# Loads of the first batch and of the first feed-forward tile on two queues, in another order

## The chip, the cores and the metric

The kernel runs on one core of a Trainium2 chip. Its engines work side by side, each through its own list of instructions in order: TensorE (PE; its weight loads are shown apart as PEld), VectorE (DVE), ScalarE (ACT), GpSimd (POOL) and SyncE (SP), which here only issues transfers. Transfers issued by SyncE and by GpSimd go through two queues to the same 16 DMA engines. The metric is the device time of one execution in microseconds: a median of 380.05 us over 8 runs, from 379.4 to 381.84.

## What is computed

Attention with a bias over 8 batches, 8 heads, 576 positions and 64 columns, then a gated feed-forward block over the 4,608 tokens that it gives (`d_model` 512, `d_ff` 1536).

```python
scores = scale * np.matmul(q, k.transpose(0, 1, 3, 2))
cum = np.cumsum(np.maximum(s, 0.0), axis=-1)
bias = -(cum[:, :, :, None] - cum[:, :, None, :])
scores = np.where(causal, -1000000000.0, scores + np.minimum(bias, 0.0))
attn = np.exp(scores - np.max(scores, axis=-1, keepdims=True))
attn = attn / (np.sum(attn, axis=-1, keepdims=True) + 1e-09)
x = np.matmul(attn, v)                 # tokens x (heads * columns)
g = x @ w_gate
out = (g * (1.0 / (1.0 + np.exp(-g))) * (x @ w_val)) @ w_out
```

## The kernel before, in words

**Attention.** Work on q and k goes by half batches of 4 heads (`HB`, 16 of them). A half batch is loaded in fp32 (`load_one`, L151: 576 KB each for k and for q), cast to bf16 (`cast_one`, L249; in two halves for half batch 0, `cast_half`, L258) and transposed into the tile `kq`: for half batches 0 to 4 (`NPE` 5) by TensorE (`pe_transpose`, L291, and the copies out of PSUM in `pe_out`, L315), for the rest through a scratch tensor in HBM and a transposing load (`scratch`, L268; `transposes`, L277; `split`, L282). The bias enters the scores as four further rows of `kq`, loaded from the tile `HL` (`aug`, L192, line L197), which is made from `s` by a scan on VectorE (L236 to L242). `kq` has two buffers, taken in turn.

A head's scores are nine products in four pieces (`score_piece`, L350, product L375). ScalarE takes the exponential into `pt` (L388), GpSimd then zeroes what lies above the diagonal by two selects (L391, L396). The values are 15 products (`av_piece`, L403, L413); `av_out` (L421) normalises into `ot`, and for batches 0 and 1 (`XB` 2) TensorE transposes a pair of heads into `XT` (`x_pe`, L456), later batches go through HBM (`x_out`, `x_in`). V is loaded in five parts (`load_v`, L166, rows of 256 B, one fp32 buffer) and cast by `cast_v` (L177).

In batch 0 the four pieces of a head are written into two PSUM tiles of two banks (`wide`), so that two activations of 1,024 and 576 columns serve a head. After batch 0 PSUM is laid out anew as eight single banks (`second_psum`, L134) and each piece has its own activation. `take` and `give` hand out the bank that was released longest ago.

**Feed-forward.** Nine tiles of 512 tokens. `gate_value` (L619) runs over 12 blocks of 128 columns: four gate products (L626), a tanh on ScalarE (L631), a product on VectorE into `pp` (L633), four value products (L641) and the product into `ht` (L649). The first two tiles then run `down_plain` (L664, product L670): four times 12 products. From tile 2 on `down_seven` (L689) saves an eighth of the products with sums of operands. The weights come as bf16 by casting loads of GpSimd (`w_load`, L331, line L342), each matrix in two halves.

**Order.** Everything is written in order by hand. L855 to L928 is batch 0: casts, transposes and bias of half batch 0, then `first_batch`, where the weight loads are issued after heads 1, 4 and 5, the loads of half batches 3 to 5, of V of batch 1 and of the down weights after head 7, and the values of head 0 and 1 after head 6, all others after head 7. `keep_warm` (L877) issues products whose results are not used. From L955 on, the loop over tiles takes one item of the feed-forward after the other, counting `n`; `hook` (L948) puts the preparation of half batches 2 and 3 at given `n`, `pump` advances the attention items (`attn_items`, L546) to a position that grows with `n`, from `n0` on, and `do_later` puts out copies of `split` that were deferred. Within `attn_items`, `side` (L481) and `side_v` (L523) put loads, casts and scratch writes at given heads and pieces, `PREP_AT`, `AV_AT` and `X_AT` the transposes, values and outputs.

SyncE's queue holds all plain loads, the scratch traffic, and the bias rows of half batches 0, 2 and 3; GpSimd's the weights, the other bias rows, the outputs and `xs`.

Of the kernel before, what the change touches and what calls it, by code (L numbers as in the profile page):

```python
# [19 lines left out]
def kernel(  # L20
# [86 lines left out]
    PTP = {0: first, "bufs": 8}  # L107

    with tc.manual_schedule():
# [3 lines left out]
        first_psum = ExitStack()  # L113
        psa = first_psum.enter_context(tc.tile_pool(name="psa", bufs=1, space=PSUM))
        bank = {}
        for i in range(2):
            bank["w", i] = psa.tile([128, 1024], FP32, name=f"wide{i}")
        for i in range(4):
            bank["s", i] = psa.tile([128, 512], FP32, name=f"one{i}")
        released = {key: i - 8 for i, key in enumerate(bank)}  # L120
# [3 lines left out]
        def take(kind="s"):  # L124
            b = min((x for x in bank if x[0] == kind), key=lambda x: released[x])
            assert released[b] < OPEN
            released[b] = OPEN
            return b
# [5 lines left out]
        def second_psum():  # L134
            assert all(x < OPEN for x in released.values())
            at_end = dict(released)
            first_psum.close()
            psb = ctx.enter_context(tc.tile_pool(name="psb", bufs=1, space=PSUM))
            bank.clear()
            released.clear()  # L140
            for i in range(8):
                bank["s", i] = psb.tile([128, 512], FP32, name=f"bank{i}")
                released["s", i] = at_end["w", i // 2] if i < 4 else at_end["s", i - 4]

# [6 lines left out]
        def load_one(hb, name, rs=(0, NR)):  # L151
# [3 lines left out]
            nc.sync.dma_start(  # L155
# [10 lines left out]
        def load_v(b, cs):  # L166
# [3 lines left out]
            for c in cs:  # L170
                n = 128 if c < 4 else TAIL
                nc.sync.dma_start(
                    t[0:n, c, :, :],
                    v[b, :, c * 128 : c * 128 + n, :].rearrange("h p d -> p h d"),
                )
# [10 lines left out]
        NEGS2 = -1.0058441162109375  # L186

# [22 lines left out]
        load_qk(1)  # L210
# [6 lines left out]
        make_identity(nc, ident)  # L217

# [10 lines left out]
        pads(0)  # L229
        init_vt(0)  # L230
        init_vt(1)
        nc.vector.memset(aug_rows(1, 0), 0.0)
        nc.gpsimd.memset(aug_rows(1, 1), 0.0)
# [114 lines left out]
        scs = {}  # L348

        def score_piece(bh, ci):  # L350
            hb, hh = divmod(bh, HB)
            pair = bh < H
            if ci == 0:
                pts[bh] = PTP[0].tile(
                [128, PTW], BF16, tag="pt", bufs=PTP["bufs"], name="pt"
            )
# [3 lines left out]
            if pair:  # L360
                if ci % 2 == 0:
                    bs = take("w")
                    scs[bh] = bs
                else:
                    bs = scs[bh]
                base = (512, 0, 0, 512)[ci]
            else:
                bs = take()
                base = 0
            o = base  # L370
            n = sum(hi - lo for _, lo, hi in CHUNKS[ci])
            sc = view(bs, 1024 if pair else 512)
            for (tj, lo, hi) in CHUNKS[ci]:
# [5 lines left out]
                    start=True,  # L379
                    stop=True,  # L380
                )
                o += w
            if not pair or ci % 2 == 1:
                if pair:
                    c0, W = ((576, 1024), (0, 576))[ci // 2]
                else:
                    c0, W = CHUNK_PT[ci], n
                nc.scalar.activation(pt[:, c0 : c0 + W], sc[:, 0:W], AF.Exp, scale=0.125)  # L388
                give(bs)
            if ci == (1 if pair else 0):  # L390
# [90 lines left out]
        def side(h, step, ci):  # L481
            bh = HB * h + step
            if bh == H + 3 and ci == 1:
                for c in range(5):
                    cast_v(1, c, nc.gpsimd)
            if h >= 3 and h + 3 < NHB and (step, ci) == (0, 1):
                load_qk(h + 3)
            hb = h + 1
            if NPE <= hb < NHB:
                late = hb == NPE  # L490
                if (step, ci) == (0, 1):
                    if late:
                        transposes(hb)
                    aug(hb, GP4)
                first = 1 if hb < NPE + 2 else 0
# [4 lines left out]
            if NPE <= hb < NHB:  # L500
                late = hb == NPE
                if (step, ci) == ((1, 1) if late else (0, 2)):
                    cast_one(hb, "k", nc.scalar)
                if (step, ci) == ((2, 1) if late else (1, 2)):
                    cast_one(hb, "q", nc.scalar)
                if (step, ci) == ((3, 1) if late else (2, 0)):
                    scratch(hb)
                if (step, ci) == (3, 3 if hb == NPE + 1 else 0) and not late:
# [5 lines left out]
            if 2 <= bn < B:  # L514
# [5 lines left out]

        V_AT = {(1, 0): 0, (2, 0): 1, (2, 2): 2, (3, 0): 3, (3, 2): 4}

        def side_v(h, step, ci):  # L523
            bn = h // 2 + 1
            if 2 <= bn < B and h % 2 == 1 and (step, ci) in V_AT:
                cast_v(bn, V_AT[step, ci], nc.scalar if bn > 2 else nc.gpsimd)

        def prep_one(hb, i):
# [3 lines left out]
            for r in range(2):  # L532
                pe_out(hb, nm, g, r, nc.scalar if nm == "k" else nc.vector)

        PREP_AT = {
            2: {(0, 3): 0, (1, 3): 1, (2, 1): 2, (2, 3): 3},
# [5 lines left out]
            H + 5: (H + 2, H + 3), H + 6: (H + 4, H + 5), H + 7: (H + 6,),  # L542
        }
        X_AT = {H + 3: (), H + 5: (H + 1,), H + 6: (H + 3,), H + 7: (H + 5,)}

        def attn_items():  # L546
            for kk in range(H, BH + 2):
                h, step = divmod(kk, HB)
                if kk < BH:
# [5 lines left out]
                    if step == 0 and 3 < h + 1 < NPE:  # L555
# [62 lines left out]

        def gate_value(tt, hps, sus):  # L619
            xt = XT[:, :, (tt % 3) * TT : (tt % 3 + 1) * TT]  # L620
            for ft in range(NFT):
                j, f0 = divmod(ft * 128, WCH)
# [384 lines left out]
```

The softmax here doesn't subtract the row's maximum and nothing guards it: scores larger than these inputs give would overflow.

## Time and profile before

| what | us |
|---|---|
| median of 8 runs | 380.05 |
| the profiled execution's own time | 380.15 |
| its span, first to last instruction | 378.3 |
| first bias rows landed | 10.95 |
| first exponential of batch 0 | 12.06 |
| first gate product of tile 0 | 32.21 |
| first values of batch 1 | 55.9 |

The granted TensorE clock is 1.00 over the whole span. The page gives for each engine its busy time, its share of the span and the count of its instructions; a row of digits shows the busy share of 40 slices of 9.46 us in tenths. The chain of waits follows the work that ended last from step to step: start, length, and the engine, tile and line. A line that begins with DMA is the flight of a transfer. In the DMA view q0 is GpSimd's queue and q1 SyncE's; their lines give packets, MB and the share of 16 engines' time.

### The profile page before, as it was taken

To read this page: it belongs to the slowest core of one execution; us is meant where nothing else is said; L and a number is where in the kernel's file an instruction comes from. 1 tells how busy PE (TensorE), PEld (TensorE's weight loads), DVE (VectorE), ACT (ScalarE), POOL (GpSimd) and SP (SyncE) were. 2 spreads that over 40 slices of the span, in tenths; PEclk is the share of its full clock that TensorE was granted. 3 is DMA by queue.
4 is the path that set the end of the run, shared out by engine and by line. 5 is a ranking of instruction groups with operands and counts; after the bars stand their busy time and mean duration, and the time that the engine had idled before them with its cause. 6 is when DMAs were issued, how large, how long until landed. Compare 5 with 4: busy or idle time off the path is not lost.

```text
span 378.3 us, 8674 instructions
## 1 busy us (share of the span) xinstructions
PE 363.1 (96%) x3246; PEld 230.4 (61%) x3246; DVE 290.3 (77%) x577; ACT 242.3 (64%) x459; POOL 206.5 (55%) x326
## 2 busy tenths in 40 slices
PE   3879999999999999999999999999999999999996
PEld 2666556655555555865586558655875575466465
DVE  7666786557895899769975998589958876985984
ACT  7686788687977777578767885697365523323321
POOL 7584357455364646595558656775675426224320
PEclk9999999999999999999999999999999999999999
DMA  7999999998488996499759665996233023001103
GB/s 251 192 248 263 199 265 268 321 267 173 159 169 272 233 282 187 119 237 295 187 164 284 200 161 159 234 201 158 49 71 114 22 30 128 0 2 68 43 2 111
DMA packets 100729, 64.22 MB, mean 170 GB/s; under 512 B 81888, under 2 KB 85824, under 8 KB 100688
## 3 DMA queue, kind: packets, MB, share of 16 engines
q1 hardware_dynamic: 91248, 46.15, 49.2%
q0 software_dynamic: 9440, 17.53, 18.4%
q8 instruction: 25, 0.41, 0.4%
q14 instruction: 16, 0.13, 0.1%
HBM read 37.90 MB, written 19.86 MB: 153 GB/s over the span
## 4 chain that ended last, share of the span: by engine, by line
PE 85%; DVE 7%; DMA 3%; ACT 2%; issue 1%; DVEq 0%; ACTq 0%; SPq 0%
PE bank L626 22%; PE bank L641 22%; PE bank L711 17%; PE bank L375 9%; PE bank L413 6%; PE bank L670 5%; PE wide L375 2%; DVE pp L633 2%; DVE ht L649 1%; ACT pt L388 1%; DMA xs<-ot 1%; DVE kq L326 1%; PE one L413 1%; DMA kq<-HL 1%; DMA s_sb<-in_s_dram 1%
## 5 line engine op out<-in xcount | busy, mean ns | idle before, releaser
L388 ACT ACTIVATE pt<-bank 128x512 bf16<-128x512 f32 x224 | 106.7, 507 | 26.3 <-PE bank L375 18.1
L626 PE MATMUL bank<-XT,wg 128*128 128x512 bf16 x432 | 110.9, 379 | 0.6 <-DVE pp L633 0.2
L641 PE MATMUL bank<-XT,wv 128*128 128x512 bf16 x432 | 110.9, 379 | 0.0
L631 ACT ACTIVATE th<-bank 128x512 bf16<-128x512 f32 x108 | 64.7, 599 | 58.8 <-PE bank L626 56.9
L633 DVE SCALAR_TENSOR_TENSOR pp<-th,bank 128x512 bf16<-128x512 bf16 x108 | 73.7, 682 | 23.8 <-ACT th L631 23.2
L649 DVE SCALAR_TENSOR_TENSOR ht<-pp,bank 128x512 bf16<-128x512 bf16 x108 | 74.0, 686 | 10.4
L658 POOL TENSOR_TENSOR ht<-ht 128x512 bf16<-128x512 bf16 x35 | 40.4, 1154 | 53.0 <-DVE su L656 52.9
L375 PE MATMUL bank<-kq 128*128 128x128 bf16 (+4 forms) x504 | 67.5, 240 | 0.2 <-DVE ht L649 0.2
L375 PEld LDWEIGHTS <-kq 128*128 128x128 bf16 x576 | 47.0, 100 | 33.0 <-issue 5.1
L641 PEld LDWEIGHTS <-wv 128*128 128x128 bf16 x432 | 38.3, 98 | 35.3
L626 PEld LDWEIGHTS <-wg 128*128 128x128 bf16 x432 | 38.4, 98 | 35.1 <-issue 1.1
L391 POOL TENSOR_SCALAR_AFFINE_SELECT pt<-pt 128x512 bf16<-128x512 bf16 x64 | 41.4, 647 | 32.8 <-ACT pt L388 32.1
L413 PEld LDWEIGHTS <-pt 128*128 128x128 bf16 x960 | 41.0, 98 | 16.6 <-issue 0.7
L413 PE MATMUL bank<-vt,pt 128*128 128x65 bf16 x840 | 41.8, 194 | 0.5 <-DVE ot L430 0.5
L447 POOL DMA_DIRECT2D xs<-ot x24 | 21.7, 906 | 28.1 <-DVE ot L430 28.1
L711 PEld LDWEIGHTS <-ht 128*128 128x128 bf16 x336 | 31.2, 98 | 4.3
L197 POOL DMA_DIRECT2D kq<-HL x52 | 32.1, 619 | 0.1
L430 DVE TENSOR_TENSOR ot<-bank,rc 128x320 bf16<-128x320 f32 x56 | 27.5, 492 | 1.9
L396 POOL TENSOR_SCALAR_AFFINE_SELECT pt<-pt 128x64 bf16<-128x64 bf16 x64 | 17.2, 269 | 18.9 <-ACT pt L388 18.8
L711 PEld LDWEIGHTS <-su 128*128 128x128 bf16 x252 | 23.6, 98 | 3.3
L670 PE MATMUL bank<-wo,ht 128*128 128x512 bf16 x96 | 24.7, 379 | 0.0
L776 POOL TENSOR_TENSOR ysb<-ysb 128x512 f32<-128x512 f32 x12 | 15.2, 1270 | 15.3 <-DVE ysb L770 15.3
(96 smaller groups left out, 397.7 us busy)
## 6 DMA issues: line engine op xcount, KB each, us to landing
rawk<-in_k_dram SPq DMA_DIRECT2D x15, 576.0 KB
rawq<-in_q_dram SPq DMA_DIRECT2D x15, 576.0 KB
rawv<-in_v_dram SPq DMA_DIRECT2D x32, 256.0 KB
out_dram<-ysb POOLq DMA_DIRECT2D x32, 256.0 KB, 3.8
xs<-ot POOLq DMA_DIRECT2D x24, 160.0 KB, 3.9
ks<-ck SPq DMA_DIRECT2D x11, 288.0 KB
qs<-cq SPq DMA_DIRECT2D x11, 288.0 KB
wg<-in_moe_w_gate_dram POOLq DMA_DIRECT2D x2, 768.0 KB, 11.7
```

The lines of the kernel that those rows point to most:

```text
L375: nc.tensor.matmul(sc[:, o : o + w], T[:, 1, e * S + 128 * tj : e * S + 128 * (tj + 1)], T[:, 0, e * S + lo : e * S + hi], start=True, sto ...
L388: nc.scalar.activation(pt[:, c0 : c0 + W], sc[:, 0:W], AF.Exp, scale=0.125)
L391: nc.gpsimd.affine_select(pt[:, 1088:1600], pt[:, 1088:1600], pattern=[[0, 4], [1, 128]], compare_op=ALU.is_ge, fill=zreg, base=0, channel ...
L413: nc.tensor.matmul(av[:, bi * (D + 1) : (bi + 1) * (D + 1)], pt[:, c0 : c0 + 128], VT[b % 2][:, tj, h, :], start=(tj == 0), stop=(tj == bi),)
L626: nc.tensor.matmul(pg, WG[j][:, c, f0 : f0 + 128], xt[:, c, :], start=(c == 0), stop=(c == 3),)
L631: nc.scalar.activation(th, pg, AF.Tanh, scale=0.5)
L633: nc.vector.scalar_tensor_tensor(pp, in0=th, scalar=1.0, in1=pg, op0=ALU.add, op1=ALU.mult)
L641: nc.tensor.matmul(pv, WV[j][:, c, f0 : f0 + 128], xt[:, c, :], start=(c == 0), stop=(c == 3),)
L649: nc.vector.scalar_tensor_tensor(hp[:, 2 * k2 : 2 * k2 + 2, :].rearrange("p a n -> p (a n)"), in0=pp, scalar=0.5, in1=pv, op0=ALU.mult, op ...
L658: (nc.vector if ft == NFT - 1 else nc.gpsimd).tensor_sub(hp[:, 1:3, :], hp[:, 1:4:2, :], hp[:, 0:3:2, :])
L670: nc.tensor.matmul(py, hps[ft // 2][:, 2 * (ft % 2) + half, c0 : c0 + 128], WO[ft // WKO][:, ft % WKO, :], start=(ft == 0), stop=(ft == NF ...
L711: nc.tensor.matmul(ps, lhs(p), rhs(p), start=(first and p == 0), stop=(last and p == NP - 1), skip_group_check=True,)
```

## The change

Loads: q of half batch 1, the first two parts of V of batch 0, k and q of half batches 2 and 3 are issued by GpSimd, between its casts; the bias rows of half batch 1 go to SyncE. The value weights of the first half and both matrices' second halves come in quarters. The down weights are issued at items 12 and 14 of tile 0. V of batch 1 and half batches 4 and 5 follow on SyncE after the bias rows of half batch 3. V of batch 1 is cast one head later, and V of batch 2 is loaded in one go later.

Batch 0: the eight single banks hold from the start. The mask of a head is a product of the identity with a tile `lower` that holds -32768 above the diagonal, accumulated under pieces 0 and 3, and the two selects are gone; four activations serve a head. The values of heads 0 to 4 stand between the scores of heads 4 to 7, and the first three blocks' gate products over three of four rows of `XT` stand ahead of the last pair's transposes. Warm-up products: 32 at the start and twice 10 before the scores, one bank (`spare`) is theirs; those at the end are gone.

Tile 0: preparation of half batch 2 from items 1 to 4 to items 3 to 6, with the second copy of each transposed group one item later (`seconds`); the attention starts at item 7, not 6; the down projection first runs over the first six blocks for all four token groups, then over the other six. Later: casts, scratch write and transposing load of half batch 5 later, values of batch 2 one head later, other items for the deferred copies in tile 2.

```diff
-    PTP = {0: first, "bufs": 8}
+    PTP = {0: first, "bufs": 7}
+    lower = first.tile([128, 512], BF16)
...
-        load_qk(1)
+        load_one(1, "k")
...
+        nc.gpsimd.memset(lower, 0.0)
+        nc.gpsimd.affine_select(
+            lower, lower, pattern=[[0, 4], [1, 128]],
+            compare_op=ALU.is_ge, fill=nc.gpsimd.to_reg(MASKED), base=0, channel_multiplier=-1,
+        )
...
+            masked_here = masked and ci in (0, 3)
+            if masked_here:
+                nc.tensor.matmul(
+                    sc, ident, lower[:, 0:n], start=True, stop=False, skip_group_check=True
+                )
...
-            if bh == H + 3 and ci == 1:
+            if bh == H + 4 and ci == 1:
                 for c in range(5):
                     cast_v(1, c, nc.gpsimd)
-            if h >= 3 and h + 3 < NHB and (step, ci) == (0, 1):
+            if bh == H + 4 and ci == 3:
+                load_v(2, range(5))
+            if h == 4 and (step, ci) in ((0, 1), (2, 1)):
+                load_qk(6 + step // 2)
+            if h >= 5 and h + 3 < NHB and (step, ci) == (0, 1):
                 load_qk(h + 3)
...
+                if late and (step, ci) == (0, 1):
+                    scratch(hb)
+                if late and (step, ci) == (0, 3):
+                    transposes(hb)
...
+            eng = nc.scalar if nm == "k" else nc.vector
+            pe_out(hb, nm, g, 0, eng)
+            seconds.append(lambda: pe_out(hb, nm, g, 1, eng))
 
         PREP_AT = {
-            2: {(0, 3): 0, (1, 3): 1, (2, 1): 2, (2, 3): 3},
+            2: {(2, 0): 0, (2, 2): 1, (3, 0): 2, (3, 2): 3},
...
+            2 * H + 1: (), 2 * H + 2: (2 * H, 2 * H + 1),
...
+            order = [(ts_, j) for ts_ in range(4) for j in range(NWCH)]
+            if tt == 0:
+                order.sort(key=lambda x: x[1])
+            for ts_, j in order:
+                yield from part(ts_, j)
...
+        keep_warm(32)
         cast_half(0, "k", 0, nc.scalar)
         cast_half(0, "q", 0, nc.scalar)
         aug(0, SP4)
-        load_v(0, range(5))
-        load_qk(2)
...
+        row_half("k", 0, nc.scalar)
+        row_half("q", 0, nc.vector)
+        cast_half(0, "k", 1, nc.scalar)
+        cast_half(0, "q", 1, nc.gpsimd)
+        load_one(1, "q", eng=nc.gpsimd)
+        load_v(0, (0, 1), nc.gpsimd)
+        load_v(0, (2, 3, 4))
+        nc.gpsimd.memset(aug_rows(1, 1), 0.0)
+        aug(1, SP4)
+        keep_warm(10)
+        row_half("k", 1, nc.scalar)
+        row_half("q", 1, nc.vector)
+        keep_warm(10)
+        cast_one(1, "k", nc.vector)
+        cast_one(1, "q", nc.vector)
+        for c in range(3):
+            cast_v(0, c, nc.gpsimd)
+        w_load("g", 0)
+        cast_v(0, 3, nc.gpsimd)
+        w_load("v", 0, 0)
+        cast_v(0, 4, nc.gpsimd)
+        for nm in ("k", "q"):
+            load_one(2, nm, eng=nc.gpsimd)
+        w_load("v", 0, 1)
+        for nm in ("g", "v"):
+            w_load(nm, 1, 0)
+        load_one(3, "k", eng=nc.gpsimd)
+        scores(0)
+        half_batch("k")
+        scores(1)
+        half_batch("q")
+        scores(2)
+        scores(3)
...
+        aug(2, SP4)
+        cast_one(2, "k", nc.gpsimd)
+        cast_one(2, "q", nc.gpsimd)
+        load_one(3, "q", eng=nc.gpsimd)
+        for nm in ("g", "v"):
+            w_load(nm, 1, 1)
+        init_vt(1)
+        scores(4)
+        values(0, 1)
+        scores(5)
+        values(2, 3)
+        scores(6)
+        values(4)
+        x_pe(0, nc.vector)
+        scores(7)
+        aug(3, SP4)
+        load_v(1, range(5))
+        load_qk(4)
+        load_qk(5)
+        values(5)
+        x_pe(1, nc.vector)
+        values(6)
+        x_pe(2, nc.scalar)
+        values(7)
+        for ft in range(3):
+            products("g", ft, XT[:, :, 0:TT], range(3))
+            if ft == 0:
+                x_pe(3, nc.scalar)
+        give(spare)
...
+        for i in range(4):
+            at_item(3 + i, prep_one, 2, i)
+        at_item(11, cast_one, 3, "k", nc.gpsimd)
+        at_item(12, cast_one, 3, "q", nc.gpsimd)
+        at_item(12, w_load, "o", 0)
+        at_item(14, w_load, "o", 1)
...
-            n0 = 6 if tt == 0 else 0
+            n0 = 7 if tt == 0 else 0
...
-                if i >= 2 * NFT or i % 4 == 1:
+                if i >= 2 * NFT or (i % 4 == 1 if tt != FIRST7 else i % 4 == 3 and i > 3):
                     do_later(1)
+                while seconds:
+                    seconds.pop(0)()
```

`scores(h)` runs the four pieces of a head, `values(*hs)` `av_piece` and `av_out` of each head, `row_half` and `half_batch` the transposes and copies of a half of half batch 0 and of k or q of half batch 1, and `products` begins a block's gate or value products or goes on with those begun.

## The prediction

> **What bounds it now.** I read the page's shares first, then the slices, then the chain of waits in order of time, then the DMA view by window, and last the landings that the trace's semaphore events give. Profiled execution: span 378.3 us, time 380.15 us, 0.10 us above the median of 380.05; so a change of the span carries over to the median as it is.
>
> ```profile
> PE 363.1 (96%) x3246; PEld 230.4 (61%) x3246; DVE 290.3 (77%) x577; ACT 242.3 (64%) x459; POOL 206.5 (55%) x326
> ...
> PE   3879999999999999999999999999999999999996
> ...
> DMA  7999999998488996499759665996233023001103
> ```
>
> TensorE is full from the fourth slice (from about 38 us) to the end, and the DMA engines are full from the second slice to the ninth (9.5 to 85 us). So only the first 35 us hold much TensorE time to win, and there a second resource, the DMA engines, is full as well. Laying each matmul's columns against the distance of the starts, TensorE stands without work for 24 us between its first and last matmul, 13 of them before 32 us; later the only gaps above 0.2 us are 0.34, 0.37, 0.38 and 0.26 us between 32 and 50 us, and 0.28 and 0.63 us at 136 to 138 us.
>
> ```profile
> 7.92 3.02 DMA kq<-HL
> 10.95 0.05 issue
> 10.99 1.05 PE wide L375 x6
> 12.04 0.02 issue
> 12.06 1.03 ACT pt L388
> ...
> 17.44 1.03 ACT pt L388
> 18.47 0.04 issue
> 18.51 0.62 PE wide L375 x6
> ...
> 31.52 0.65 ACT XT L468
> 32.17 0.04 issue
> 32.21 1.04 PE bank L626 x4
> ```
>
> Here the reader sees the start as three links: the bias rows arrive (10.95), eight heads of exponentials run on ScalarE (12.06 to 27.57, a new head every 1.71 us with one hole of 1.9 us), then a tail of values, outputs and transposes until tile 0's first gate product (32.21).
>
> **Part by part. Bias rows.** By the semaphore events k1 landed at 9.60 us, q1 at 11.03 and head 0's bias rows at 10.95: the bias packets waited behind q1, on the same queue. The change issues q1 from GpSimd after GpSimd's cast (8.23 to 8.89), so the bias waits for k1 alone: 9.7 instead of 10.95. TensorE must still pass the second half's transposes (q's cast ends at 8.89; nine of them took 1.17) and ten warm-up matmuls (0.6), which ends near 10.2, and the first exponential then starts at 10.8 instead of 12.06. **-1.25** (ends: -0.2 if the transposes keep their first speed, -1.5).
>
> **Heads.** Four activations of one head in separate banks took 1.69 us (start of the first to end of the last, row at 39.95 us) against 1.71 for two wide ones: nothing. The mask as a matmul adds 576 columns per head, 0.24 us by 0.216 us for 512, 1.9 us in all; ScalarE hides it, busy 9.39 of 10.16 us from 17.44 to 27.6, while TensorE's part of one head (1,600 columns, 0.67, and the mask, 0.24) fits in 1.7 us. Without that cover it would cost 1.9. GpSimd is rid of sixteen selects in batch 0 (8 x (0.63 + 0.23) = 6.9 us), which pays for ten more issues of 0.6 to 0.9 us each (seven loads and three more pieces of weights; four bias rows go to SyncE, at 0.62 each there, with no load behind them until heads 0 to 3 are scored). Holes: k1's cast (0.76) comes behind the copies of q's second half on VectorE, then 18 transposes of 56 ns (1.0) stand before head 1, about 0.9 us; the five casts of V (0.61 each) all on GpSimd, behind the landings, end near 19.3 where head 0's values could start at 18.5, 0.8 us; q1 on GpSimd's queue 0.3. Together 2.0 against 1.9 now: nothing. The exponentials end at 26.4.
>
> **Tail.** Values of heads 0 to 6 now lie between the scores. After the last exponential come 0.57 us of values (row L413 x15) and then nine gate products (0.216 each, 1.94), beside which the last pair's reciprocal, product, transposes and copy run (0.2 + 0.5 + 0.36 + 0.65 = 1.7). So gate work starts near 27.1, not 32.21: **-5.1**, the 1.25 included. What is late next is a load, below.
>
> **Tile 0.** The four gaps of 32 to 50 us (1.35) ended with VectorE (`pp`, `ht`), which the two copies of each transposed group (1.46 to 1.65) hold up; the change puts the second copy behind the next item and starts the group two items later. I take **-0.7** (0 to -1.35). At 136 us the copies of `pk` stand ahead of `rc`; they move by two items: **-0.5** (0 to -0.9). Starts together: -6.3.
>
> **The loads that then decide.** The same bytes must come in, and what is needed 5 us earlier must land 5 us earlier. Gate and value weights move from before head 2 to behind V's casts; k2, q2, k3, q3 and the halves of the weights go through GpSimd's queue; batch 1's V stays on SyncE, now behind the last bias rows (heads 4 to 7 must be scored), about 24 us. The DMA view from 39 to 48 us shows how two queues share:
>
> ```profile
> q0 software_dynamic: 1349, 1.40, 90.8%
> q1 hardware_dynamic: 1349, 0.34, 29.0%
> ```
>
> Packet for packet: V's packets of 256 B get one turn for every weight packet. So V of batch 1 (4,608 packets) lands when GpSimd's queue has sent about as many. Counted from 24 us: k2, q2, k3, q3 1,024, six weight halves 3,072 (512 rows each), then down weights 768 a part. Packet times, from the trace: 0.134 us for a weight row of 768, 0.096 for one of 512, so about 0.077 for one of 384; 0.1 for k and q; 0.021 for V; sixteen engines. The 4,096 packets then take (4096 x 0.021 + 3072 x 0.077 + 1024 x 0.1)/16 = 26.6 us, to 50.6, and the 512 left take (0.096 + 0.021) x 512/16 = 3.7: V's last part lands at 54.3, is cast at 54.9. Now it lands at 54.5 and the values that need it run at 57.1, which less 5.1 is 52.0: a wait of about **+3.0**. It stands on TensorE's queue ahead of gate and value products, so it counts in full. The ends: 0, if gaps in GpSimd's stream let V through (V alone moved a part of 1,024 packets in 1.2 us); 8.7, if two half rows travel as one packet, since V then gets half the turns and ends only behind the second part of the down weights, near 60. I take 3.0, the count by rows sent singly, as the trace's weight rows are.
>
> [...]
>
> **Costed at nothing.** Down projection of tile 0 by halves: the same 48 products of 0.216; needed because the second part of the weights, issued 14 items into the tile, lands near 60 to 65, where the first halves (24 products and what is interleaved) end near 66; cover gone, up to 3 us. Half batch 5's scratch write goes a head later (heads 15 and 16 are 4.4 us apart) and its transposed reads wait for it; now they land at 78.4 and 80.4, for head 20 at 89.3; 0 to +2, taken as 0, as 4 us remain. Batch 2's V and values each move by a head: no gap stands there now.
>
> **Sum.** -5.1 - 0.7 - 0.5 + 3.0 = -3.3: 376.8 us.
>
> **Rivals.** (a) *No load is late.* For it: now V's last three parts landed in 2.5 us once GpSimd's queue was empty, and any pause there does the same. Then -6.3: 373.8. (b) *The loads rule altogether.* For it: the DMA engines are full from 10 to 85 us and the change leaves them idle for 2 to 3 us (9.6 to 10.6, and between V and the gate weights, whose first packet came 4.5 us after their issue at 16.05). V then lands 3 us later still, 6 us of wait: -0.3, 379.8, no change. (c) *V starves*, the case on the other side: two half rows to a packet, V lands near 60.2, cast at 60.9 against 52.0, a wait of 8.7 in the fifth head of batch 1; sum +2.4: 382.5. It decides from a landing at 57.7 on. Against it: the weight rows of now travel singly, those of 2 KB too. (d) The change may not do what it says: if GpSimd's casts wait so long that the gate weights land after 28 us, tile 0 starts later, each us costing one; that ends in (b).
>
> **Numbers.** Forecast 0.45; (a) 0.25; (b) 0.12, with (d); (c) 0.18. An interval of 0.3% is 1.1 us, about what a measurement of this kernel can tell from no change; so faster 0.70, same 0.12, slower 0.18. Range: from (a) with all gaps of tile 0 and of 136 us gone (372.8), a little below, 372.3, up to 382.5, the bound of V's wait. The forecast's own range is 374.5 to 378.5.
>
> **What would show it.** Right: `kq<-HL` of head 0 landing before 10 us; the last exponential of batch 0 near 26.4; first L626-type product near 27; a wait of TensorE for `vt` in head 12, some 3 us long, with V's last part landing near 54; TensorE then without gaps to the end. Wrong: gate products waiting for `wg` or `wv` (weights in the wrong order), TensorE waiting for `kq` at head 20 (scratch too late), or no wait at head 12 at all, which would be (a).

## The result and the profile after

The changed kernel takes 384.59 us (median of 11 runs, 384.08 to 386.71), the kernel before 380.3 beside it: a ratio of 1.0112, 95% interval 1.0088 to 1.0136. It is 4.3 us slower, where 3.3 us less were forecast. The profiled execution took 384.65 us with a span of 382.9 (before: 380.15 and 378.3). Its twelve executions, the profiled one among them, differ by TensorE's mean granted clock: eight with 0.998 or more took 384.08 to 384.87 us, four with 0.991 to 0.996 took 385.62 to 386.71.

First the page's shares and slices of the changed kernel, in the places that were shown of before.

```profile
PE 366.1 (96%) x3300; PEld 231.6 (60%) x3300; DVE 292.3 (76%) x577; ACT 242.8 (63%) x473; POOL 208.1 (54%) x320
...
PE   7699879998999999999999999999999999999995
...
DMA  6899999899669997599659965895123113001103
```

TensorE's busy time is 3.0 us longer: the masks add 2.1 us and the warm-up 3.8, and all other products take 2.9 less. These 2.9 are won at the start. Before, TensorE took 0.83 ns a column up to 17.6 us (nine transposes 1.17 us) and 0.42 from there on; in the changed kernel, with its 32 warm-up products, the faster rate begins at 6.1 us (nine transposes 0.69). (The trace of the kernel before has no clock record ahead of 17.6 us, and its view's 1.00 holds from there on alone.) The shares barely move, and the slices of 9.57 us say where to look: the fifth and sixth (38 to 57 us) and the tenth (86 to 96) have fallen below 9. Next the chain of waits of the changed kernel (start, length, what).

```profile
3.02 5.24 DMA rawq<-in_q_dram
...
8.39 0.60 POOL cq L255
9.00 5.21 DMA rawq<-in_q_dram
...
14.24 0.77 DVE cq L245
...
16.21 0.47 ACT pt L368
16.68 3.56 DMA kq<-HL
...
21.04 0.63 POOL vt L168
...
53.42 0.63 DVE kq L315
54.05 0.04 issue
54.09 0.40 PE bank L358 x4
54.49 0.02 issue
54.51 0.61 ACT pt L368
55.12 0.06 issue
55.18 0.63 POOL pt L373
55.81 2.24 POOL vt L168 x4
```

The link `kq<-HL` at 7.92, the first of before, is gone: head 0's bias rows landed at 9.51 us by the semaphore events, the first exponential began at 10.94 (before 10.95 and 12.06). In its place stands a flight of q of half batch 1, 5.21 us long, which GpSimd issued; it landed at 14.21, where before it landed at 11.03. Its transposes stand ahead of head 2's scores on TensorE's queue, so these wait for it; later the values wait for V's casts on GpSimd (to 21.66). Then comes a piece that before has none of: copies of transposed q on VectorE up to 54.05, head 12's scores, its exponential, its select on GpSimd, and only behind the select the five casts of V of batch 1, which the values then wait for. The waits of TensorE add these up (line, releaser, us in total, times, longest):

```profile
PE bank L358 <- DVE kq L315: 3.3, 2, 2.0
...
PE bank L286 <- DVE cq L245: 1.1, 1, 1.1
PE bank L358 <- DVE kq L273: 1.0, 1, 1.0
PE bank L395 <- POOL vt L168: 1.0, 2, 0.7
...
PE bank L286 <- DVE ck L245: 0.9, 1, 0.9
```

The two largest are heads 8 and 12 (gaps of 1.51 us to 39.56 and 2.14 to 54.09); the one of 1.0 is head 20 (1.20 to 91.73). Before, no gap from 32 to 130 us was above 0.4.

To place gain and loss in time I laid the two traces over each other by useful work: the columns of all matmuls except masks and warm-up, added up in order, and the time at which each kernel has done the same sum. The **lead** of the changed kernel is +2.2 us where tile 0 starts (30.8 us), +1.5 at 50, -1.2 at 59 (heads 8 and 12, V's casts), -2.4 at 98 (head 20), -3.7 at 161, -4.1 at 191, -4.3 at the end. Between 98 and 161 us stand the deferred copies of tile 2.

**Theories.** 1: the loss is one of order on engines: VectorE's copies, and GpSimd's casts, stand right ahead of what needs them. 2: it is one of loads: GpSimd's queue brings them too late, and later losses follow from that whatever the order. Both are read place by place.

### The profile page after: what moved, and what is told of

Read it like the earlier page. It is cut to its first block, busy times and chain, and to the rows that moved or that the text cites. A ratio compares the mean times of both kernels' runs of the same rounds, so it can differ in the third digit from the quotient of the medians.

```text
span 382.9 us, 8798 instructions
## 1 busy us (share of the span) xinstructions
PE 366.1 (96%) x3300; PEld 231.6 (60%) x3300; DVE 292.3 (76%) x577; ACT 242.8 (63%) x473; POOL 208.1 (54%) x320
## 4 chain that ended last, share of the span: by engine, by line
PE 81%; DVE 8%; DMA 6%; ACT 2%; POOL 1%; issue 1%; SPq 1%; DVEq 0%; ACTq 0%; POOLq 0%
PE bank L627 43%; PE bank L726 16%; PE bank L358 10%; PE bank L395 7%; PE bank L677 3%; DMA rawq<-in_q_dram 3%; DMA XT<-xs 2%; DVE ht L654 2%; DVE pp L643 2%; DVE kq L273 1%; DVE kq L315 1%; DMA kq<-HL 1%; POOL vt L168 1%; PE bank L445 1%; DVE ot L412 1%
## 5 line engine op out<-in xcount | busy, mean ns | idle before, releaser
L368 ACT ACTIVATE pt<-bank 128x512 bf16<-128x512 f32 (+1 forms) x256 | 120.5, 507 | 35.1 <-PE bank L358 24.3
L654 DVE SCALAR_TENSOR_TENSOR ht<-pp,bank 128x512 bf16<-128x512 bf16 x108 | 74.1, 686 | 10.8 <-PE bank L358 0.5
L358 PE MATMUL bank<-kq 128*128 128x128 bf16 (+4 forms) x576 | 74.9, 240 | 4.5 <-DVE kq L315 3.3
L663 POOL TENSOR_TENSOR ht<-ht 128x512 bf16<-128x512 bf16 x35 | 40.4, 1155 | 51.5 <-DVE su L661 51.5
L358 PEld LDWEIGHTS <-kq 128*128 128x128 bf16 x576 | 45.5, 98 | 34.2 <-issue 4.8
L373 POOL TENSOR_SCALAR_AFFINE_SELECT pt<-pt 128x512 bf16<-128x512 bf16 x56 | 36.5, 651 | 32.6 <-ACT pt L368 32.1
L395 PE MATMUL bank<-vt,pt 128*128 128x65 bf16 x960 | 46.9, 194 | 1.9 <-POOL vt L168 1.0
L412 DVE TENSOR_TENSOR ot<-bank,rc 128x320 bf16<-128x320 f32 x64 | 31.5, 492 | 2.2
L183 POOL DMA_DIRECT2D kq<-HL x48 | 29.2, 610 | 0.0
L677 PE MATMUL bank<-wo,ht 128*128 128x512 bf16 x96 | 25.9, 379 | 0.0
L378 POOL TENSOR_SCALAR_AFFINE_SELECT pt<-pt 128x64 bf16<-128x64 bf16 x56 | 15.6, 279 | 18.7 <-ACT pt L368 18.5
L411 DVE RECIPROCAL rc<-bank 128x5 f32<-128x5 f32 x64 | 12.1, 189 | 14.9 <-PE bank L395 14.4
```

Of the source, the lines that this page charges most:

```text
L358: nc.tensor.matmul(sc[:, o : o + w], T[:, 1, e * S + 128 * tj : e * S + 128 * (tj + 1)], T[:, 0, e * S + lo : e * S + hi], start=not maske ...
L368: nc.scalar.activation(pt[:, c0 : c0 + n], sc, AF.Exp, scale=0.125)
L373: nc.gpsimd.affine_select(pt[:, 1088:1600], pt[:, 1088:1600], pattern=[[0, 4], [1, 128]], compare_op=ALU.is_ge, fill=zreg, base=0, channel ...
L395: nc.tensor.matmul(av[:, bi * (D + 1) : (bi + 1) * (D + 1)], pt[:, c0 : c0 + 128], VT[b % 2][:, tj, h, :], start=(tj == 0), stop=(tj == bi),)
L412: nc.vector.tensor_mul(ot[:, :, e * D : (e + 1) * D], av3[:, :, 0:D], rc[:, :, None].to_broadcast([128, NCH, D]),)
L654: nc.vector.scalar_tensor_tensor(hp[:, 2 * k2 : 2 * k2 + 2, :].rearrange("p a n -> p (a n)"), in0=pp, scalar=0.5, in1=pv, op0=ALU.mult, op ...
```

## Experiments

Each compares with the kernel before on the same chip. "Span" is that of the profiled execution.

**1. Tile 2's copies at their old items.**

```diff
-if i >= 2 * NFT or (i % 4 == 1 if tt != FIRST7 else i % 4 == 3 and i > 3):
+if i >= 2 * NFT or i % 4 == 1:
```

> The changed kernel with one line put back: in tile 2 the deferred copies go out at the same items as in the kernel before. Theory 1 (the time is lost where VectorE's copies stand right ahead of what needs them): the gaps of 0.76, 0.53, 0.24 and 0.20 us at 139 to 151 us shrink to about the 0.9 us of the kernel before, 383.6 us. Theory 2 (the loads of GpSimd's queue land too late, and every later loss follows from it): no change, 384.6.

384.11 us, ratio 1.0124 (1.0098 to 1.0149), span 381.5, that is 1.4 less. The ratio alone shows no gain. But two of the four executions had a mean clock of 0.994; the two at 0.998 took 383.21 and 383.53, 0.9 less than the eight of the changed kernel in the middle. The lead is 1.5 us better from 161 us on, 1.0 of it won in tile 2 and the rest ahead of it. First the changed kernel's copies on VectorE, then GpSimd beside them, then VectorE in this run:

```profile
136.60 1.43 DVE L273 COPY kq<-pk 64x1152 bf16<-64x1152 bf16 x1
...
142.10 1.33 DVE L273 COPY kq<-pk 64x1152 bf16<-64x1152 bf16 x1
```
```profile
136.56 1.15 POOL L663 TENSOR_TENSOR ht<-ht 128x512 bf16<-128x512 bf16 x1 [0.65 <-DVE su L661]
...
141.97 1.15 POOL L663 TENSOR_TENSOR ht<-ht 128x512 bf16<-128x512 bf16 x1 [3.25 <-DVE su L661]
```
```profile
134.03 0.96 DVE L273 COPY kq<-pk 64x1152 bf16<-64x1152 bf16 x1
...
138.46 0.71 DVE L273 COPY kq<-pk 64x1152 bf16<-64x1152 bf16 x1
```

The new items put both copies beside GpSimd's product of operands, where the same copy takes 1.33 to 1.43 us. In the edited run the two take 0.96 and 0.71, 1.1 us less of VectorE's time: order, Theory 1.

**2. Half batch 3's transposes sooner.**

```diff
-2: {(2, 0): 0, (2, 2): 1, (3, 0): 2, (3, 2): 3},
+2: {(2, 0): 0, (2, 1): 1, (2, 2): 2, (2, 3): 3},
```

> The changed kernel with half batch 3's four transposed groups after pieces 0 to 3 of head 10, instead of pieces 0 and 2 of heads 10 and 11. Theory 1: the 2.1 us gap ahead of head 12's scores goes, as the copies on VectorE end some 2 us sooner; with the casts of V behind that head's select, up to 2.5 us in all, 382.1 to 382.6. Theory 2: k3 and q3 (landed at 42.0 and 43.7) and their casts on GpSimd (to 45.6) are the limit, TensorE then waits at the earlier place instead, 384.6 or slower.

383.74, ratio 1.0102 (1.0087 to 1.0118). The gap of 2.14 us is gone. Behind it the values wait 0.50, 0.47 and 0.44 us for V's casts (57 us): GpSimd still has them behind head 12's select. One wait had covered another.

**3. Half batch 5's deferred copies sooner.**

```diff
-first = 2 if late else 1 if hb < NPE + 3 else 0
+first = 1 if hb < NPE + 3 else 0
```

> The changed kernel with the copies of half batch 5 put on the list one head sooner (heads 17 and 18 instead of 18 and 19). Theory 1: the 1.2 us gap ahead of head 20's scores goes, 383.4. Theory 2: the transposed loads (landed at 80.5 and 82.2) are the limit, the wait moves to VectorE ahead of the copies, 384.6.

385.22, ratio 1.0141 (1.0111 to 1.017): the wait of 1.20 ahead of head 20 went, and 0.66 came ahead of a gate product at 82.7. The lead is 0.5 better at that place, the time not better.

**4. Batch 0's q and V back on SyncE.**

```diff
-load_one(1, "k")
+load_qk(1)
...
-load_one(1, "q", eng=nc.gpsimd)
-load_v(0, (0, 1), nc.gpsimd)
-load_v(0, (2, 3, 4))
+load_v(0, range(5))
```

> The changed kernel with q of half batch 1 back at the start of SyncE's queue and all of V of batch 0 on SyncE behind the first bias rows. Theory 2: q1 lands near 11 instead of 14.2 us, the holes of ScalarE ahead of heads 2, 4 and 5 shrink by about 3 us while the first exponential starts 1.2 us later, so tile 0 starts 1 to 2 us sooner and the end comes with it, 382.6 to 383.6. Theory 1: tile 0 may start sooner, but heads 8 and 12 wait for the same copies, so less than half of it arrives at the end, 384 to 384.6.

382.98, ratio 1.0085 (1.0069 to 1.01). Tile 0's start has a lead of 3.6 us instead of 2.2. But the profiled execution lost it again at head 12: in windows around that wait of 2.14 us, the fields PE busy and PEclk (the granted clock) read

```profile
52.00:53.00 1.00, 0.38 (x5) 0.32 (x5) 0.57 (x1) 0.09 (x1) 0.24 (x1) 1.00 1.11 298
53.00:54.00 1.00, 1.00 (x6) 0.45 (x4) 0.00 (x0) 0.60 (x1) 0.30 (x1) 0.82 1.13 305
54.00:55.00 1.00, 1.00 (x3) 0.30 (x2) 0.32 (x1) 0.60 (x1) 1.00 (x3) 0.50 1.15 276
55.00:56.00 1.00, 1.00 (x5) 0.48 (x4) 0.97 (x2) 0.00 (x0) 1.00 (x3) 0.50 1.12 297
56.00:57.00 1.00, 1.00 (x6) 0.49 (x4) 0.81 (x2) 0.88 (x2) 1.00 (x3) 0.50 1.12 293
57.00:58.00 1.00, 1.00 (x15) 0.63 (x14) 0.00 (x0) 0.40 (x2) 0.12 (x1) 0.97 1.16 293
```

that TensorE ran at half its clock from 53.65 us on for 3.41 us: four value products in a row took 1.91 us instead of 1.03. In the changed kernel the same wait left the clock at 1.00. Three of the four executions of this run have a mean clock of 0.994 or 0.995; the fourth took 382.55 us.

**5. Experiment 2 with V's casts sooner.** The casts of V of batch 1 at `bh == H + 3 and ci == 3`, not `bh == H + 4 and ci == 1`.

> Changed kernel with the transposes of half batch 3 sooner, as in the run with those alone, and the casts of V of batch 1 issued in head 11 instead of head 12, so that they stand ahead of head 12's select on GpSimd. Theory 1 (order on the engines): the wait of 2.1 us ahead of head 12's scores and the 1.4 us of waits of values for the casts are both gone; the lead over the kernel before, -1.2 us at the work where the changed kernel stands at 59 us, becomes +0.5 to +1.5, and of that 1.5 to 2.7 us reach the end: 381.9 to 383.1. Theory 2 (loads set the pace): V of batch 1 lands at 51 us and half batch 5 as late as now, the gain is waited away ahead of heads 12 to 20, and the time stays within 0.5 us of 384.6.

383.18, ratio 1.0081 (1.005 to 1.0112), span 380.6, 2.3 less. The lead at that work is +0.8 instead of -1.2, a gain of 2.0 that the end keeps, as Theory 1 has it. A wait of 0.44 for the casts was left.

**6. Four mends together** (1, 4 and 5).

> The same, with the deferred copies of tile 2 at their old items, and q of half batch 1 and the first two parts of V of batch 0 on SyncE's queue again. Theory 1: the terms add up. Tile 0 starts 1.4 us sooner (loads on SyncE), heads 12 to 14 win 2.5, tile 2 wins 1.0 to 1.5, the waits ahead of head 8 (1.5) and head 20 (1.2) stay: 4.9 to 5.4 less than the changed kernel, 379.2 to 379.7 and at the worst 380.5, so about the time of the kernel before. Theory 2: what is won early is waited away at half batch 5, whose reads land when they do now; only tile 2 and the end remain, 382 to 383.

379.24, ratio 0.9972 (0.9957 to 0.9988), span 377.1, 5.3 us less than the changed kernel, within the 4.9 to 5.4 expected. The three parts alone had taken 0.5, 1.6 and 1.4 us off the median, 3.5 in all; whether the rest is noise or a wait that one mend uncovers and another removes isn't shown. TensorE's waits on VectorE's copies and GpSimd's casts are now

```profile
PE bank L358 <- DVE kq L315: 1.4, 1, 1.4
...
PE bank L358 <- DVE kq L273: 1.0, 1, 1.0
...
PE bank L395 <- POOL vt L168: 0.3, 1, 0.3
```

heads 8 and 20, as expected, and a rest at V. The lead is +4.3 at tile 0's start and +1.35 at the end; the other runs with the same start (4, 7 to 9, 12, 13 and 15 to 17) have 3.3 to 3.8 there.

**7 and 8. Attention an item later in tile 0** (`n0 = 8`), **and half batch 5's copies sooner** (edit 3), each on top of experiment 6.

> As the run with four mends, and the attention in tile 0 starts one item later (8, not 7), so that half a block more of gate or value products stands between the last transposes of half batch 2 and head 8's scores. If the wait of 1.5 us ahead of head 8 is one of order on TensorE's queue (Theory 1): it shrinks by about the 0.86 us of four products, and the time is 0.5 to 0.9 us below the run with four mends. If VectorE is simply full there (products and copies 8.6 us in 8), the wait moves on behind head 8 and the time does not change.

379.13, ratio 0.9966 (0.995 to 0.9982): no change. Head 8's wait fell from 1.51 to 0.66, but 0.52 came ahead of a value product at 51.5, on VectorE's `pp`, and values waited 0.92 instead of 0.27 at 69.5.

> As the run with four mends, and the deferred copies of half batch 5 one head sooner. In the changed kernel alone that moved 0.5 us at its place. Theory 1: the 1.2 us ahead of head 20 go, some 0.7 come back as a wait ahead of a gate product, 0.3 to 0.8 us below the run with four mends. Theory 2: with more lead the scratch reads of half batch 5 (74.9 and 76.2 us) are themselves late, and the time is the same or up to 1 us longer, as VectorE then waits for them with its other work behind.

379.91, 0.9976 to 1.0046: no gain. The wait ahead of head 20 became one of 1.42 at 80 us: VectorE stood for the transposed reads of half batch 5.

**9. Half batch 5's chain sooner**: on top of 6, its casts in heads 14 and 15, scratch write at the end of head 15, reads at the start of head 16, edit 3, and V's casts at `H + 3, ci == 1`.

> As the run with four mends, with the casts of V of batch 1 half a head sooner (from its 11th head's second piece), and half batch 5's chain as a whole sooner: casts in heads 14 and 15, scratch write at the end of head 15, transposed reads at the start of head 16, deferred copies from head 17. Theory 1 (order): the 0.6 us of waits of values for V's casts near 54 us and the 1.2 us ahead of head 20 both go, with nothing in their place: 377.2 to 377.9, against 379.24 with four mends. Theory 2 (half batch 5's loads, landed 59.9 and 62.6 us there, and the scratch traffic behind them are the limit): a wait of about 1.2 us shows again, as it did at 80 us with the copies alone sooner, and the time stays at 378.4 to 379.4.

379.17, ratio 0.9971 (0.9953 to 0.9989), the time of experiment 6. The waits for V's casts are gone, the one for half batch 5 is not. VectorE of this run, then of experiment 16:

```profile
77.38 1.44 DVE L273 COPY kq<-pk 64x1152 bf16<-64x1152 bf16 x2 [2.43 <-DMA pk<-ks]
78.85 0.46 DVE L452 COPY XT<-bank 128x576 bf16<-128x576 bf16 x1
```
```profile
74.50 1.26 DVE L273 COPY kq<-pk 64x1152 bf16<-64x1152 bf16 x2
76.85 0.46 DVE L452 COPY XT<-bank 128x576 bf16<-128x576 bf16 x1 [1.09 <-PE bank L445]
```

In the first, VectorE waits 2.43 us for `pk`, and the copy into `XT`, which the next gate product needs, stands behind. `pk` landed at 77.36 though its scratch write had landed at 69.61, 3.1 us sooner than in experiment 6 (72.75, `pk` 77.82). Here Theory 1 fell and a form of Theory 2 stood.

**10. Without masks.**

> The changed kernel without the mask products of batch 0; the entries above the diagonal stay in, so batch 0's output differs. The prediction took the 1.9 us of mask products as hidden by ScalarE's exponentials. If so, the first gate product of tile 0 moves by less than 0.4 us from 29.26 and the time by less than 0.4 from 384.6. If TensorE sets batch 0's pace instead, both move by up to 1.9.

384.57, ratio 1.0117 (1.0083 to 1.0151): the masks cost nothing that the time shows, and 0.4 us at tile 0's start, where the lead is +2.6 against +2.2.

**11. Down projection whole.** `order.sort` left out.

> The changed kernel with tile 0's down projection as before, twelve products to a token group in one go, not by halves. The second part of the down weights lands at 65 us. The prediction took the halves as needed and free, up to 3 us without them. If needed: a new wait of TensorE for the weights between 58 and 65 us and a time 1 to 3 us above 384.6. If the attention items beside it cover the wait, or the weights are there: within 0.4 of 384.6.

385.06, ratio 1.0132 (1.0094 to 1.0169), the same within what can be told, with no wait for the down weights. The halves cost nothing and weren't needed.

**12. Preparation of half batch 2 an item sooner**, on top of 9.

> As the run with half batch 5 sooner, and the preparation of half batch 2 in tile 0 from items 2 to 5 instead of 3 to 6, both groups of k first and then both of q. Theory 1: the wait of 1.5 us ahead of head 8's scores is there because VectorE makes its last copies for it right before; an item sooner is 0.86 us, so the wait falls to 0.5 to 0.8 and the time by 0.7 to 1.0 against the run with half batch 5 sooner. Theory 2: k and q of half batch 2 land at 29.0 and 30.6 us and their casts end near 30.2 and 31.8, so the transposes wait for them instead, at items 2 and 4, and the time is the same or up to 0.5 longer.

379.85, ratio 0.9996 (0.9979 to 1.0013): head 8's wait grew from 1.52 to 2.07. With both groups of k first, VectorE's copies of q came last of all, the final two from 37.02 and from 39.20. Moving them sooner by items didn't move them ahead of their user.

**13. Tile 1's copies at other items**, on top of 9.

```diff
-i % 4 == 1
+(i % 2 == 1 and i > 2 if tt == 1 else i % 4 == 1)
```

> As the run with half batch 5 sooner (379.17), with the deferred copies of tile 1 at other items: none at item 1, then one at every second item, where there was one at every fourth item. In that run VectorE stood from 74.95 to 77.38 for the reads of half batch 5 (pk landed at 77.36), two of their copies ran at once, and the copy into XT behind them kept TensorE waiting for 1.43 us. Theory 1 (order): with XT's copy ahead of them and one copy at a time, no wait above 0.4 us is left between 78 and 92 us, and the time is 0.9 to 1.4 us less: 377.8 to 378.3. Theory 2 (the reads land too late for whatever needs them): about 1.2 us of wait shows once more, ahead of head 20 or of a product, and the time stays within 0.4 of 379.2.

379.32, ratio 0.9974 (0.9952 to 0.9996). It tests nothing: the two copies are put out at the end of tile 0, not in tile 1, and stayed ahead of `XT`'s. The wait was 2.0 us in the profiled execution, and TensorE ran at clocks of 0.59 and 0.55 in the two windows of 2 us behind it.

**14. Only q of half batch 1 back on SyncE.**

> The changed kernel with q of half batch 1 back on SyncE's queue at the start, and V of batch 0 left as the change has it (two parts on GpSimd). With both loads on SyncE tile 0's start came 1.4 to 2.0 us sooner at equal work. Theory 1: it is q alone that counts, since V's casts were held by k's and q's place in the DMA engines; tile 0's start is 1.2 to 2.0 us sooner, the time 383.0 to 383.5. Rival: it is V's parts on two queues (packets of 256 B against packets of 512 B and more); then tile 0's start moves by less than 0.6 and the time stays above 383.9.

383.45, ratio 1.0083 (1.0057 to 1.0108): 1.1 us below the changed kernel, and tile 0's start has a lead of 3.3. So q is most of what experiment 4 won, 1.1 of the 1.4 us of lead there. That V's parts are the rest isn't shown: the ratios of the two runs, 1.0083 and 1.0085, are the same.

**15. Two late copies of q of half batch 2 on ScalarE**, on top of 13.

> As the run with the copies of tile 1 at other items, with the two late copies of q of half batch 2 on ScalarE instead of VectorE, which has 2.1 of 4 us busy there against VectorE's 3.4. Theory 1: the wait of 1.5 us ahead of head 8 ends with VectorE's copies; two of 0.7 us less leave 0.2 to 0.6 of it, and the time falls by 0.9 to 1.3 us against that run. Rival: ScalarE's tanh for the products then comes later, and the wait goes to the value products' side: the time is the same within 0.4.

380.85, ratio 1.0006 (0.9979 to 1.0032), runs from 378.37 to 383.2. Head 8's wait fell to 0.73, but the lead won went into a wait of 2.98 at 79.8, for reads that landed when they had before (77.29), with TensorE at half clock behind it (0.50 from 80 to 82 us). The wide spread goes with that clock: the four executions with a mean clock of 0.998 or more took 378.37 to 378.90 us, the seven with 0.995 or 0.996 took 380.38 to 382.22, the one with 0.991 took 383.2.

**16. Reads of half batch 5 ahead of the loads of half batch 6** on SyncE's queue, on top of 9; half batch 6's casts and scratch write move half a head later too.

```diff
-if h == 4 and (step, ci) in ((0, 1), (2, 1)):
+if h == 4 and (step, ci) in ((0, 3), (2, 1)):
     load_qk(6 + step // 2)
```

> As the run with half batch 5 sooner (379.17), but the transposed reads of half batch 5 stand ahead of the loads of k and q of half batch 6 on SyncE's queue (loads half a head later, their casts and scratch write half a head later too). So far the reads landed at 77.3 to 77.8 us however early their scratch write was (69.2 to 73.5), always behind the same loads on the same queue, each 1.7 to 2.1 us. Theory 2 for this place (the queue's order): pk then lands near 74, before VectorE reaches its copies, the 1.4 us of wait at 79.4 goes, no wait above 0.4 is left between 70 and 92 us, and the time is 0.9 to 1.4 us less, 377.8 to 378.3. Theory 1 for this place (only the order of VectorE's copies): pk's landing does not matter and 1.2 us or more of wait shows as before, 379.2.

378.01, ratio 0.9945 (0.9925 to 0.9965), about 1.1 us below experiment 9 (1.0 by the ratios). `pk` landed at 71.87 and VectorE took it without a wait (lines above). TensorE has no wait on an engine between 70 and 92 us. The queue's order it was: half batch 5's reads had stood behind two loads of 576 KB that nobody needed yet.

**17. The same, with the two copies on ScalarE.**

> The same, with the two late copies of q of half batch 2 on ScalarE. In the earlier run with these copies the wait ahead of head 8 fell from 1.52 to 0.73 us, and the lead won (0.8 to 1.2) was lost again at 80 us, where pk landed no sooner. With pk sooner it should stay: 0.7 to 1.1 us below the run with reads before loads, 376.8 to 377.5. If something else holds the pace there (V of batch 2, the scratch itself): the same time as that run.

377.44, ratio 0.9933 (0.9906 to 0.996), span 375.3, 7.1 us below the changed kernel; the 0.6 us against experiment 16 lie within the intervals. Its remaining waits after batch 0 begin with

```profile
PE bank L358 <- DVE kq L315: 0.6, 1, 0.6
PE bank L395 <- DVE ot L412: 0.5, 1, 0.5
```

and of the lead of 3.3 at tile 0's start 3.0 are left in the span at the end. This version beats both kernels.

## Why the prediction was wrong, step by step

**Bias rows, -1.25: right in size, and worth little.** The first exponential came 1.12 us sooner. But experiment 14 began its exponentials at 12.39, later than the kernel before (12.06), and still had a lead of 3.3 at tile 0's start. The clock has a part in what was won at the start, too, and the reading of the profile missed it: of the 13 us before 32 us that were taken as TensorE without work, some 5 were products at half rate (0.83 ns a column). No run separates the two.

**Heads, 2.0 against 1.9: failed.** The step named the waits (k's and q's casts, V's casts) but priced q's move at 0.3 and V's casts as done by 19.3. q landed 3.2 us later than before, because a transfer that GpSimd issues at 9.00 had its first packet at 10.61 and then shared the engines with V; the casts ended at 21.66. TensorE waits 1.1 + 0.9 + 0.7 us, and the last exponential ended at 28.27, not 26.4. That masks hide was right to 0.4 us (experiment 10).

**Tail, -5.1: right in kind, too large.** The first gate product came at 29.26, not 27.1, and at equal work 2.2 us were won. With q and V on SyncE it was 3.3 to 3.8 in nine runs and 4.3 in experiment 6. So the loads' move took 1.1 to 2.1 away, and the reordering of values and gate products falls 0.8 to 1.8 short of what was said of it. The forecast took the time of the first gate product for the gain; but that product now stands ahead of the last pair's transposes, so that in experiment 6, where it came at 27.22 as forecast, 5.0 us sooner than before, the lead at equal work was only 4.3.

**Tile 0, -0.7: wrong sign.** I looked at where VectorE was late before, and not at who needs the second copy that was moved behind the next item. It is the next half batch's first scores, on TensorE's queue ahead of everything: 1.51 and 2.14 us of wait for 1.35 removed, and with V's casts behind them a lead of +2.2 became -1.2. Two copies moved to ScalarE take 0.8 off the first (experiments 15 and 17), other items for the transposes take away the second (experiment 2).

**136 us, -0.5: wrong sign.** The new items put the copies beside GpSimd's product, and the two waits became several, 1.0 us worse in tile 2 (experiment 1).

**V's wait, +3.0: the wrong wait.** V landed at 51.06, sooner than computed (54.3). The equal shares that were counted on did come, some 185 packets a us on each queue from 43 to 46 us; but k and q travelled as 512 packets of 4,608 B, not 1,024, and in the two us from 47 on GpSimd's queue sent only 66 and 49 packets and V 780 and 730. (Equal counts show equal shares; they don't show that the turns are of single packets, since equal groups give the same.) But V's casts had been put behind head 12's select on GpSimd, and that one waited for scores that waited for VectorE. I had asked what was queued behind TensorE's wait, not ahead of GpSimd's cast. Rival (a) was right that no load of batch 1 is late, and its time was wrong by more, 10.8 us.

**Half batch 5, taken as 0 with an end of +2: 1.2.** The 4 us of slack that I counted were given to VectorE's copies, put half a tile later, right ahead of head 20; once those are moved, the reads' place in SyncE's queue decides (experiments 9 and 16).

**Down projection, 0: right**, and needless (experiment 11).

So the sum, of the 7.6 us between -3.3 and +4.3: 2.9 are the tail, which stood at +2.2 instead of +5.1 of lead. Heads 8 and 12 cost 3.4 where tile 0 and V together had stood at 2.3; that only 1.1 is wrong there is luck, as the forecast's one wait stood in for two that it did not see. Head 20 is 1.2, and from there to the end 1.9 were lost where 0.5 was to be won, 2.4. Rival (c) came nearest with 382.5, by a mechanism that did not come.

Two slips in the reading change nothing: the fourth slice begins at 28.4 us, not 38, and the lower end of rival (a) adds up to 372.7, not 372.8.

By place, Theory 1 (order) held at heads 8 and 12 and in tile 2, Theory 2 (loads) at the start of batch 0 and for the reads of half batch 5.

What stays open: why `pk` landed 1.4 us behind the scratch write of q in experiment 16 and 4.4 us in experiment 6; what makes the lead at tile 0's start differ from 3.3 to 4.3 between runs with the same start; and where the 0.6 us behind tile 2 were lost, of which a wait of 0.49 for `ot` at 181 us is the largest piece. These were not tried.

## What to carry to other kernels

When an operation is put later because its engine is crowded, follow its result to the first instruction that needs it and to that instruction's place in its own queue: work moved behind one item is often moved to just ahead of the next stage. A transfer on another queue is priced from that queue's first packet (here 10.61 us for an issue at 9.00), not from the data's time, and a queue's order is checked for loads that nobody needs yet. Mend the waits together before judging: experiments 2 and 3 alone mostly uncovered the next wait, and four mends together gave 5.3 us.

## What was not expected of the hardware

The copy of 64 x 1152 on VectorE took longer beside some of GpSimd's work: in the changed kernel the 23 that ran beside no operation of GpSimd's but an issue took 0.44 to 0.48 us, the four beside selects that overlapped them for over 0.55 us in one piece 0.89 to 0.95, and the three beside its product of two tensors for over 1 us 1.33 to 1.52. No run shows why. The copy that began 0.04 us after GpSimd's product, at 136.60, ended 0.32 us behind its end, a little less than the 0.44 to 0.48 of a copy alone.

Behind a wait of 2 us TensorE's clock halved in some runs: it did behind 2.14 us in experiment 4 (0.50 for 3.41 us), behind 2.0 in experiment 13 (0.59 and 0.55 in the two windows of 2 us behind it) and behind 2.98 in experiment 15 (0.50 from 80 to 82 us), and did not behind 2.14 in the changed kernel (1.00). The profiled executions of these three experiments and of experiment 2 have a mean clock of 0.994 to 0.996, those of all other runs 0.998 to 1.00.

The two waits of 2.14 us differ in their place. In the traces of the two kernels the clock changes once, to 0.50 at the end, 110 times 3.41 us behind its first record in the changed kernel and 106 times in the kernel before. Counted off from the changed kernel's first record (6.12 us), a step of 3.41 us ends at 53.91, within the wait, and had 1.97 us without work (0.42 ns to a column counted as work). In experiment 4 the whole wait lies in the 3.41 us ahead of the change (50.24 to 53.65). That this place decides is an estimate from these two waits and these lengths; no run moved a wait alone. By it the same wait costs itself alone or, from half of 3.41, some 1.7 us more, by where it falls.
